# Batch 0's second quad of a windowed-attention kernel: own banks for its second score round, value units in two parts, and the first weight matrix loaded by 512 columns

## Chip, cores and metric

The kernel runs on one core of a Trainium2 chip. The metric is device microseconds (us) of one execution; of several executions the median counts. All inputs and the output lie in HBM, and the whole computation is one launch.

## What is computed

Two stages. The first is an attention of 8 batches x 8 heads, head size 64, with 512 local and 32 global positions. A local query sees the 32 global keys and the local keys at most 32 positions away; a global query sees everything. The second is a gated feed-forward over the 4352 resulting rows of 512 features.

```
s_g   = scale * q_g @ concat(k_g, k_l).T ;  out_g = softmax(s_g) @ concat(v_g, v_l)
s_ll  = scale * q_l @ k_l.T, kept where |i - j| <= 32 ;  s_lg = scale * q_l @ k_g.T
out_l = softmax(concat(s_lg, s_ll)) @ concat(v_g, v_l)
x     = concat(out_g, out_l), heads side by side: (8 * 544) x 512
h     = x @ w_in            # 512 x 2048
g     = h * sigmoid(1.702 * h)
out   = g @ w_out           # 2048 x 512
```

## The kernel before, in words

**Tiling.** Four heads of a batch form a quad, each head on 32 of the 128 partitions (its 64 features as pairs of bf16). Every batch has two quads; `a` is the first and `c` the second. Scores are computed keys by queries in four chunks of 128 keys; chunks 0 and 1 are score round 0, chunks 2 and 3 are round 1. In batch 0 the mask is added on TensorE: `B` (L327) multiplies a bias by an identity into the score banks, and `S` (L337) adds the scores of local keys to it. `gk` (L364) gives scores of global keys: for the global queries (32 columns) and, in `K` (L388), for all local queries (a bank of its own, `kb`). ScalarE takes the exponentials: `X` (L374) of the score banks, `XK` (L413) of `kb`. Then come three value units: unit 0 multiplies by ones (the denominators), units 1 and 2 by the two halves of the values. `ekU` (L417) opens a unit with the global keys, `U` (L428) adds the four local chunks. `Gm` (L443) does the global queries' rows, `eg` (L394) prepares its last operand. `R` (L459) turns the denominators into reciprocals on VectorE (transpose, reciprocal, transpose), and `XL` (L469) multiplies a value unit by them into `xL`, the feed-forward's input: quad `a` fills k chunks 0 and 1 of `xL`, quad `c` chunks 2 and 3. `G` (L472) finishes the global rows.

**Feed-forward.** `h_mm` (L582) multiplies a 128-column block `fc` of `w_in` (16 blocks, 4 k chunks each) by `xL`. Batch 0's first four blocks stand in one group of four banks: chunks 0 and 1 of all four first (L709), then, behind quad `c`'s `XL`, chunks 2 and 3 (L713). `tanh2`, `act4` and `h_step` (L595) follow, with Tanh on ScalarE and a multiply on VectorE. `o_mm` (L602) multiplies by `w_out`.

**PSUM.** There are eight banks. Four belong to the pool `psP` (L63), handed out in turn by `pbank` (L276): a new holder waits until the old holder's readers are done. The other four are two tiles of two banks each, `s0` and `s1`, handed out together by `spair` (L280); `bank(pair, j)` (L283) is one of the four. A pair of banks is one tile.

**Order.** The order on every engine is written out by hand; each engine runs its own list in order and waits where an operand or a buffer is not ready. L640 to L735 is batch 0. GpSimd (POOL) issues nearly all loads. `load_rest` (L251) is its list: values of batch 0, `w_in` as four DMAs of 512 KB (column half by column half, in each the rows of k chunks 0 and 1, then those of 2 and 3), two parts of `w_out`, six small mask copies, the loads of batch 1, two more parts of `w_out`, and so on. These DMAs share eight semaphores in turn, so each waits, before it is issued, for the landing of the eighth DMA before it. Later batches use the class `Wide` (L499) and the loop from L860, which the change does not touch.

Of the kernel before, what the change touches and what calls it, by code (L numbers as in the profile page):

```python
# [20 lines left out]
def kernel(  # L21
# [12 lines left out]
    nc = tc.nc  # L34

    B, H, Sl, D = q_l.shape
    Sg = q_g.shape[2]
    S = Sg + Sl
    n_tokens = B * S
    d_model = H * D  # L40
    d_ff = moe_w_in.shape[1]
    assert (B, H, Sl, Sg, D) == (8, 8, 512, 32, 64)
    W = 32
    scale = 1.0 / (D ** 0.5)
# [29 lines left out]
    def load(b, us=(0, 1), kq=True):  # L74
        if b not in loaded:
            loaded[b] = (ld.tile([128, 2, 16 * D], BF16, name="rk"),
                         ld.tile([128, 2, 16 * D], BF16, name="rq"))
        if kq:
            s = slice(us[0], us[-1] + 1)
            nc.gpsimd.dma_start(out=loaded[b][1][:, s], in_=qf[b][:, s])  # L80
            nc.gpsimd.dma_start(out=loaded[b][0][:, s], in_=kf[b][:, s])  # L81
# [8 lines left out]
    def load_v(b):  # L90
        if b == 2:
            nc.gpsimd.memset(v_view(b, 5)[:, :, :, :, D:], 1.0)
        vt = v_view(b, 5).rearrange("p u j c d -> p (u j) c d")
        vs, vg = (x[b].rearrange("h s d -> s h d") for x in (v_l, v_g))
        for c in range(5):
            n = 128 if c == 2 else 96
            nc.gpsimd.dma_start(out=vt[0:n, :, c, :D], in_=vs[FIRST[c] : FIRST[c] + n])  # L97
            if c != 2 and b > 1:
                nc.gpsimd.dma_start(out=vt[96:128, :, c, :D], in_=vg)  # L99

    def load_vg(b):
        nc.gpsimd.dma_start(out=v_view(b, 5).rearrange("p u j c d -> p (u j) c d")[96:128, :, 0, :D],
                            in_=v_g[b].rearrange("h s d -> s h d"))
# [16 lines left out]
    def load_g(lo, hi, names="kq"):  # L120
        for name, dst, src in (("k", rkg, kgf), ("q", rqg, qgf)):
            if name in names:
                nc.gpsimd.dma_start(out=dst[:, lo:hi, :], in_=src[:, lo:hi, :])
# [37 lines left out]
    for i in range(2):  # L161
# [3 lines left out]
        out=step, in_=step, pattern=[[1, 289]], compare_op=ALU.is_ge,  # L165
        fill=0.0, base=-97, channel_multiplier=-1,
    )
    w_in_sb = wts.tile([128, 2, NKC, d_ff // 2], BF16)
    w_out_sb = wts.tile([128, FC, d_model], BF16)
    w_in_r = moe_w_in.rearrange("(u p h) f -> u p h f", u=2, h=2)  # L170
# [30 lines left out]
    def near(t, c):  # L201
        lo = 0 if c else 2
        return t[:, :, lo : lo + WIN[c][1]]
# [13 lines left out]
    def make_mask(part):  # L217
        rnd, at, t0, t1, nr, base, rows = part
        src = band[:, base : base + 16 * nr].rearrange("p (r t) -> p t r", t=16)
        nc.gpsimd.tensor_copy(mask_at(rnd, at, t1 - t0, nr)[0:rows], src[0:rows, t0:t1])  # L220
# [19 lines left out]
    def load_v2(b):  # L240
        vp = v_l[b].rearrange("(u h) (c p) d -> u p h c d", u=2, p=128)
        for u in range(2):
            for p in (slice(0, 64), slice(64, 128)):
                nc.gpsimd.dma_start(out=v_view(b, 4)[p, u, :, :, :D], in_=vp[u, p])  # L244

    def load_w_out(g4):
        nc.gpsimd.dma_start(
            out=w_out_sb[:, 4 * g4 : 4 * g4 + 4, :].rearrange("p (g e) m -> p g (e m)", e=2),
            in_=w_out_r[:, 2 * g4 : 2 * g4 + 2, :])

    def load_rest():  # L251
        load_v2(0)
        half = d_ff // 2
        for part in range(2):
            for u in range(2):
                nc.gpsimd.dma_start(out=w_in_sb[:, part, 2 * u : 2 * u + 2, :],
                                    in_=w_in_r[u][:, :, part * half : (part + 1) * half])
        load_w_out(1)
        load_w_out(0)
        for part in MASKS:  # L260
            make_mask(part)
        load(1, (0,))
        load_g(2, 4)
        load(1, (1,))
        load_vg(1)
        load_w_out(2)
        load_w_out(3)
        load_v(1)
        load(2, (0,))
        load_g(4, 8)  # L270
        load(2, (1,))
# [4 lines left out]
    def pbank(name):  # L276
        return psP.tile([128, 512], F32, name=name, tag="p")


    def spair():  # L280
        return [psS.tile([128, 2, 512], F32, name="s4", tag="s%d" % i) for i in range(2)]

    def bank(pair, j):  # L283
        return pair[j // 2][:, j % 2, :]

    class Quad:
# [38 lines left out]


        def B(self, rnd, split=False, js=range(4)):  # L327
            if 0 in js:
                self.bk[rnd] = [pbank("s") for _ in range(4)] if split else self.spt(rnd)
            ps = self.bk[rnd] if split else [bank(self.bk[rnd], j) for j in range(4)]  # L330
            for c in (2 * rnd, 2 * rnd + 1):
                w = (40, 200, 36, 228)[c]
                for j in js:
                    nc.tensor.matmul(ps[j][:, w : w + 16 * WIN[c][1]], lhsT=ident, rhs=near(bias, c),
                                     start=(c == 2 * rnd), stop=False, skip_group_check=True)
# [49 lines left out]
            if rnd == self.gr:  # L385
                nc.scalar.activation(e[:, 2, RW:], bank(self.ps, 2)[:, RW : RW + 32], AF.Exp, scale=scale)

        def K(self, e=None):  # L388
            if e != 1:
                self.kb = pbank("kb")  # L390
            self.gk(self.kb, self.q[:, 4:20], e)


# [20 lines left out]
            self.ek = att.tile([128, Sl], BF16, name="ek")  # L414
            nc.scalar.activation(self.ek, self.kb, AF.Exp, scale=scale)

        def ekU(self, unit):  # L417
            ov = pbank("ov")
            self.st[unit] = ov
            for j in range(4):  # L420
                r = 32 * ((j + 1) % 4)
                p = slice(r, r + 32)
                lv = (ones32[p] if unit == 0 else
                      rvg[p, self.Q, :D].rearrange("p (w h) -> p w h", h=2)[:, :, unit - 1])
                nc.tensor.matmul(ov[32 * j : 32 * j + 32, :], lhsT=lv, rhs=self.ek[p],
                                 start=True, stop=False, skip_group_check=True)

        def U(self, unit):  # L428
            ov = self.st[unit]
            h = unit - 1  # L430
            for c in range(4):
                r0, nr = WIN[c]
                at = (40, 200, 36, 228)[c]
                for j in range(4):
                    lv = (ones32 if unit == 0 else
                          self.v[:, j, c, :D].rearrange("p (w h) -> p w h", h=2)[:, :, h])
                    nc.tensor.matmul(  # L437
                        ov[32 * j : 32 * j + 32, :].rearrange("p (t r) -> p t r", t=16)[:, :, r0 : r0 + nr],
                        lhsT=lv, rhs=self.E[c // 2][:, j, at : at + 16 * nr],
                        start=False, stop=(c == 3), skip_group_check=True,  # L440
                    )
# [140 lines left out]
    def h_mm(i, fc, hp, kcs):  # L582
        for kc in kcs:
            nc.tensor.matmul(hp[:, : width(i)], lhsT=w_in_c[:, fc // 8, kc, fc % 8 // 2, :, fc % 2],  # L584
                             rhs=(xL[i] if i < B else xG)[:, kc, :],
                             start=(kc == 0), stop=(kc == NKC - 1))
# [53 lines left out]
    a, c = Quad(0), Quad(1)  # L640
# [20 lines left out]
    cast_g32("k", rkg)  # L661
    transpose_g(0, 2, "k")
    load_rest()
    a.B(0)
    a.B(1, split=True)
# [8 lines left out]
    c.ext()  # L674
    c.Tk()
    c.B(0)
    a.K()
    a.XK()
    c.S(0, added=True)
    c.gg()  # L680
    c.X(0)
    a.eg()
    a.ekU(0)
    a.U(0)
    a.R()
    c.K()
    c.XK()
    a.ekU(1)
    a.U(1)
    a.XL(0)  # L690
    c.B(1, js=(0, 1))
    c.B(1, js=(2, 3))
    c.S(1, added=True)
    c.X(1)
    a.ekU(2)
    a.U(2)
    a.XL(1)
    a.Gm()
    gTs[0] = moe.tile([128, FC, TB], BF16, name="gT")
    pt = pts[0] = spair()  # L700
    c.ekU(0)
    c.ekU(1)
    c.U(0)
    c.R()
    c.U(1)
    c.ekU(2)
    c.U(2)
    c.eg()
    for fc in range(4):  # L709
        h_mm(0, fc, bank(pt, fc), (0, 1))  # L710
    c.XL(0)
    c.XL(1)
    for kc in (2, 3):  # L713
        for fc in range(4):
            h_mm(0, fc, bank(pt, fc), (kc,))
# [24 lines left out]
    a, c = nq[1]  # L740
# [28 lines left out]
    pt = spair()  # L769
# [7 lines left out]
    a, c = nq[2]  # L777
# [82 lines left out]
    for i in range(1, B):  # L860
        if i > 1:
            for fc in range(FC):
                h_step(i, fc)
        if i + 1 < B:
            phase_o(i)
# [36 lines left out]
```

## Time and profile before

| what | value |
|---|---|
| median of 3 runs | 301.46 us (301.28 to 302.13) |
| the profiled execution's own time | 302.02 us |
| its span, first to last instruction | 300.3 us |
| TensorE (PE) busy | 289.9 us (97%) |
| VectorE (DVE) busy | 219.0 us (73%) |
| ScalarE (ACT) busy | 165.1 us (55%) |
| GpSimd (POOL) busy | 78.0 us (26%) |
| mean granted TensorE clock | 0.998 |

So 1.7 us of the profiled execution lie outside the span, and that execution is 0.56 us above the median. All times inside the span count from its first instruction. In listings of the timeline each row gives the start, the length from the first start to the last end of a merged group, the engine (PEld is the weight loads of PE), the line, and how many instructions were merged; in brackets stands the idle time before the group and what ended it. Where a matmul's length is given, it is the time from its start to its modelled end; matmuls overlap, so a sequence is priced from start to start.

### The profile page before, as it was taken

To read this page: it belongs to the slowest core of one execution; us is meant where nothing else is said; L and a number is where in the kernel's file an instruction comes from. 1 tells how busy PE (TensorE), PEld (TensorE's weight loads), DVE (VectorE), ACT (ScalarE), POOL (GpSimd) and SP (SyncE) were. 2 spreads that over 40 slices of the span, in tenths; PEclk is the share of its full clock that TensorE was granted. 3 is DMA by queue.
4 is the path that set the end of the run, shared out by engine and by line. 5 is a ranking of instruction groups with operands and counts; after the bars stand their busy time and mean duration, and the time that the engine had idled before them with its cause. 6 is when DMAs were issued, how large, how long until landed. Compare 5 with 4: busy or idle time off the path is not lost.

```text
span 300.3 us, 8109 instructions
## 1 busy us (share of the span) xinstructions
PE 289.9 (97%) x3373; PEld 149.0 (50%) x3414; DVE 219.0 (73%) x446; ACT 165.1 (55%) x250; POOL 78.0 (26%) x126
## 2 busy tenths in 40 slices
PE   8889999999999999999999999999999999999994
PEld 4544446445454455445454455445554455456553
DVE  6668977979967887778967887778878866773310
ACT  4727465476547736477356745566446652663421
POOL 8942748728054001800072002500000000000000
PEclk9999999999999999999999999999999999999999
DMA  7999999994979312980289114900230022101123
GB/s 205 158 204 210 202 180 206 214 131 59 175 90 159 71 37 55 139 142 21 53 85 184 34 38 81 115 0 20 55 71 2 2 53 57 35 0 37 35 70 73
DMA packets 58373, 28.20 MB, mean 94 GB/s; under 512 B 47456, under 2 KB 47712, under 8 KB 58336
## 3 DMA queue, kind: packets, MB, share of 16 engines
q0 software_dynamic: 50496, 17.57, 51.8%
q1 hardware_dynamic: 7360, 9.45, 12.2%
q10 hardware_dynamic: 480, 0.66, 0.7%
q8 instruction: 27, 0.44, 0.6%
q14 instruction: 10, 0.08, 0.1%
HBM read 36.31 MB, written 8.91 MB: 151 GB/s over the span
## 4 chain that ended last, share of the span: by engine, by line
PE 84%; DVE 5%; DMA 4%; POOL 3%; ACT 2%; issue 1%; ACTq 0%; POOLq 0%
PE op L609 37%; PE hp L584 34%; PE s L529 6%; PE ov L555 5%; DMA w_in_sb<-in_moe_w_in_dram 4%; DVE gT L592 2%; POOL v L244 1%; ACT th L591 1%; DVE xL L470 1%; PE op L621 1%; PE s L584 1%; PE og L566 1%; DVE rs L465 0%; DVE sT L461 0%; ACT e L540 0%
## 5 line engine op out<-in xcount | busy, mean ns | idle before, releaser
L609 PE MATMUL op<-w_out_sb,gT 128*128 128x512 bf16 x497 | 119.4, 379 | 1.8 <-issue 0.3
L592 DVE SCALAR_TENSOR_TENSOR gT<-th,hp 128x512 bf16<-128x512 f32 (+1 forms) x140 | 91.0, 656 | 40.0 <-ACT th L591 38.8
L584 PE MATMUL hp<-xL,w_in_sb 128*128 128x512 bf16 x488 | 108.9, 379 | 1.3 <-DVE xL L470 0.4
L591 ACT ACTIVATE th<-hp 128x512 f32<-128x512 f32 (+1 forms) x140 | 79.7, 573 | 44.8 <-PE hp L584 40.3
L584 PEld LDWEIGHTS <-w_in_sb 128*128 128x128 bf16 x576 | 56.1, 98 | 66.9 <-issue 2.2
L609 PEld LDWEIGHTS <-gT 128*128 128x128 bf16 x528 | 49.3, 98 | 54.9
L623 ACT ACTIVATE ob<-op 128x512 f32<-128x512 f32 (+2 forms) x35 | 20.3, 587 | 67.6 <-PE op L609 65.1
L540 ACT ACTIVATE e<-s 128x1016 bf16<-128x1016 f32 (+1 forms) x56 | 53.3, 1005 | 7.4 <-PE s L529 7.1
L97 POOL DMA_DIRECT2D v<-in_v_l_dram x35 | 28.1, 809 | 92.5 <-PE og L566 88.3
L545 DVE TENSOR_TENSOR e<-e,mask 128x1712 bf16<-128x1712 bf16 (+1 forms) x27 | 28.1, 1041 | 5.2 <-ACT e L540 5.2
L461 DVE STREAM_TRANSPOSE sT<-ov 128x512 f32<-128x512 f32 x15 | 10.7, 716 | 14.9 <-PE ov L555 12.7
L470 DVE TENSOR_TENSOR xL<-ov,rs 128x512 bf16<-128x512 f32 x30 | 19.4, 686 | 1.9 <-PE ov L437 0.5
L529 PE MATMUL s<-q,kT 32*128 32x160 bf16 (+3 forms) x672 | 19.2, 243 | 0.0
L529 PEld LDWEIGHTS <-kT 32*128 32x128 bf16 x672 | 13.1, 94 | 12.0 <-issue 6.5
L99 POOL DMA_DIRECT2D v<-in_v_g_dram x24 | 14.2, 591 | 3.8 <-DMA rq<-in_q_l_dram 3.1
L503 DVE STREAM_TRANSPOSE kT<-rk 128x512 f32<-128x512 f32 x14 | 14.6, 1042 | 0.0
L465 DVE STREAM_TRANSPOSE rs<-rT 128x512 f32<-128x512 f32 x16 | 11.4, 711 | 0.6
L555 PE MATMUL ov<-e,v 128*32 128x128 bf16 (+3 forms) x624 | 11.8, 223 | 0.0
L312 DVE STREAM_TRANSPOSE q<-rq 128x512 f32<-128x512 f32 (+1 forms) x17 | 11.3, 667 | 0.1
L555 PEld LDWEIGHTS <-v 128*32 128x32 bf16 x672 | 10.5, 97 | 0.0
L584 PE MATMUL hp<-xG,w_in_sb 128*128 128x256 bf16 x64 | 9.6, 273 | 0.1
L81 POOL DMA_DIRECT2D rk<-in_k_l_dram x10 | 6.5, 648 | 3.6 <-DMA w_in_sb<-in_moe_w_in_dram 1.9
(99 smaller groups left out, 151.3 us busy)
## 6 DMA issues: line engine op xcount, KB each, us to landing
out_dram<-ob SPq DMA_DIRECT2D x132, 64.0 KB, 2.4
v<-in_v_l_dram POOLq DMA_DIRECT2D x28, 96.0 KB, 4.4
rq<-in_q_l_dram POOLq DMA_DIRECT2D x5, 512.0 KB, 7.6
rk<-in_k_l_dram POOLq DMA_DIRECT2D x5, 512.0 KB, 9.4
w_in_sb<-in_moe_w_in_dram POOLq DMA_DIRECT2D x4, 512.0 KB, 11.7
w_out_sb<-in_moe_w_out_dram POOLq DMA_DIRECT2D x4, 512.0 KB, 12.6
v<-in_v_l_dram POOLq DMA_DIRECT2D x11, 128.0 KB, 4.8
rq<-in_q_l_dram POOLq DMA_DIRECT2D x5, 256.0 KB, 8.6
```

Source lines behind the costliest of these rows:

```text
L97: nc.gpsimd.dma_start(out=vt[0:n, :, c, :D], in_=vs[FIRST[c] : FIRST[c] + n])
L470: nc.vector.tensor_mul(self.x[:, 2 * self.u + h, :], self.st[1 + h], self.st["rs"])
L503: nc.vector.transpose(flat[:, 0:Sl].rearrange("p (r t) -> p t r", t=16), loaded[self.b][0][:, self.u].bitcast(F32))
L529: nc.tensor.matmul(bank(self.ps, j)[:, at : at + n], lhsT=self.k[p, KEYS[c] : KEYS[c] + 128, e], rhs=self.q[p, lo:hi, r0 : r0 + nr, e], st ...
L540: nc.scalar.activation(self.E[rnd][:, 2 * i : 2 * i + 2, :n], self.ps[i][:, :, :n], AF.Exp, scale=scale)
L545: eng.tensor_mul(e, e, mask[:, rnd : rnd + 1, :n].to_broadcast([128, 4, n]))
L555: nc.tensor.matmul(ov[32 * j : 32 * j + 32, :].rearrange("p (t r) -> p t r", t=16)[:, t0:t1, r0 : r0 + nr], lhsT=lv, rhs=self.E[rnd][:, j, ...
L584: nc.tensor.matmul(hp[:, : width(i)], lhsT=w_in_c[:, fc // 8, kc, fc % 8 // 2, :, fc % 2], rhs=(xL[i] if i < B else xG)[:, kc, :], start=( ...
L591: nc.scalar.activation(th[:, :n], hp[:, :n], AF.Tanh, scale=0.851)
L592: nc.vector.scalar_tensor_tensor(gTs[i][:, fc, :n], in0=th[:, :n], scalar=1.0, in1=hp[:, :n], op0=ALU.add, op1=ALU.mult)
L609: nc.tensor.matmul(op, lhsT=gTs[i][:, fc, tci * 128 : tci * 128 + 128], rhs=w_out_sb[:, fc, :], start=(first and fc == 4 * f4), stop=(fc = ...
L623: nc.scalar.activation(ob[:, lo:hi], op[:, lo:hi], AF.Copy, scale=0.5)
```

## The change

It touches batch 0 and the `w_in` load only.

- `load_rest` loads `w_in` in six DMAs: columns 0 to 511 of k chunks 0 and 1, then of chunks 2 and 3 (256 KB each); columns 512 to 1023 the same way (256 KB each); then columns 1024 to 2047 in two DMAs of 512 KB as before.
- Quad `c`'s round 1 no longer uses the paired banks but four `psP` banks (`split=True`). Its bias is added in two steps: banks 0 to 2 before `a.ekU(0)`, bank 3 behind `a.U(1)`. The exponentials of that round are four instructions instead of two, and the global queries' scores are taken in round 1 (inside `S`) instead of by `gg` in round 0.
- `c.S(0)` moves ahead of `a.K`. `a`'s unit 0 goes into the bank of `a.kb`. The freed paired banks, under the new name `pt`, hold in this order: `c.kb`, `a`'s unit 1, `a`'s unit 2, `c`'s unit 0.
- Each of `c`'s value units is done in two parts: chunks 0 and 1 of all three units ahead of `a.Gm`, chunks 2 and 3 behind it. `c.R` stands behind the second part of unit 0. Both `a.XL` stand behind `a.U(2)`. `c.eg` moves behind `c.XL(1)`.

```
@@ load_rest
-        half = d_ff // 2
-        for part in range(2):
+        for part, lo, hi in ((0, 0, 512), (0, 512, 1024), (1, 0, 1024)):
             for u in range(2):
-                nc.gpsimd.dma_start(out=w_in_sb[:, part, 2 * u : 2 * u + 2, :],
-                                    in_=w_in_r[u][:, :, part * half : (part + 1) * half])
+                nc.gpsimd.dma_start(out=w_in_sb[:, part, 2 * u : 2 * u + 2, lo:hi],
+                                    in_=w_in_r[u][:, :, 1024 * part + lo : 1024 * part + hi])
@@ B
-            if 0 in js:
-                self.bk[rnd] = [pbank("s") for _ in range(4)] if split else self.spt(rnd)
+            if split:
+                self.bk.setdefault(rnd, []).extend(pbank("s") for _ in js)
+            elif 0 in js:
+                self.bk[rnd] = self.spt(rnd)
@@ K, ekU and U take a bank, or a list of chunks
-        def K(self, e=None):
+        def K(self, e=None, kb=None):
...
-                self.kb = pbank("kb")
+                self.kb = pbank("kb") if kb is None else kb
...
-        def ekU(self, unit):
-            ov = pbank("ov")
+        def ekU(self, unit, ov=None):
+            if ov is None:
+                ov = pbank("ov")
...
-        def U(self, unit):
+        def U(self, unit, cs=range(4)):
...
-            for c in range(4):
+            for c in cs:
@@ the order of batch 0
     c.B(0)
+    c.S(0, added=True)
     a.K()
     a.XK()
-    c.S(0, added=True)
-    c.gg()
     c.X(0)
     a.eg()
-    a.ekU(0)
+    c.B(1, split=True, js=(0, 1, 2))
+    a.ekU(0, a.kb)
     a.U(0)
     a.R()
-    c.K()
+    pt = spair()
+    c.K(kb=bank(pt, 0))
     c.XK()
-    a.ekU(1)
+    a.ekU(1, bank(pt, 1))
     a.U(1)
+    c.B(1, split=True, js=(3,))
+    c.S(1, split=True, added=True)
+    c.X(1)
+    a.ekU(2, bank(pt, 2))
+    a.U(2)
     a.XL(0)
-    c.B(1, js=(0, 1))
-    c.B(1, js=(2, 3))
-    c.S(1, added=True)
-    c.X(1)
-    a.ekU(2)
-    a.U(2)
     a.XL(1)
+    c.ekU(0, bank(pt, 3))
+    c.U(0, (0, 1))
+    for unit in (1, 2):
+        c.ekU(unit)
+        c.U(unit, (0, 1))
     a.Gm()
+    c.U(0, (2, 3))
+    c.R()
+    c.U(1, (2, 3))
+    c.U(2, (2, 3))
     gTs[0] = moe.tile([128, FC, TB], BF16, name="gT")
     pt = pts[0] = spair()
-    c.ekU(0)
-    c.ekU(1)
-    c.U(0)
-    c.R()
-    c.U(1)
-    c.ekU(2)
-    c.U(2)
-    c.eg()
     for fc in range(4):
         h_mm(0, fc, bank(pt, fc), (0, 1))
     c.XL(0)
     c.XL(1)
+    c.eg()
```

## The prediction

> **What bounds the kernel now.** I read the page first: PE is busy 97% of the span and carries 84% of the chain that ended last, so a change of order pays only where PE stands idle. The chain in order of time names the last such place that is not PE's or DVE's own pace, the second half of the first feed-forward block in batch 0:
>
> ```profile
> 9.99 11.03 DMA w_in_sb<-in_moe_w_in_dram
> 21.02 0.05 issue
> 21.07 1.90 PE s L584 x8
> ```
>
> The columns are start, length, what. A `w_in` load issued at 9.99 lands at 21.02, and PE goes on at 21.07. From there the chain is PE and DVE work to the end, released by each other and by no load; so a delay or gain at 21.07 goes through whole. The timeline from 8 to 29 us shows what stands ahead of it:
>
> ```profile
> 11.48 0.66 ACT L415 ACTIVATE ek<-kb 128x512 bf16<-128x512 f32 x1
> ...
> 11.96 1.74 ACT L384 ACTIVATE e<-s 128x856 bf16<-128x856 f32 x2
> ...
> 14.63 0.66 PE L351 MATMUL s<-q,kT 32*128 32x228 bf16 x16
> ...
> 15.34 1.66 ACT L384 ACTIVATE e<-s 128x856 bf16<-128x856 f32 x2 [1.06 <-PE s L351]
> ...
> 17.41 0.72 DVE L461 STREAM_TRANSPOSE sT<-ov 128x512 f32<-128x512 f32 x1 [0.63 <-PE ov L437]
> ...
> 18.59 1.67 PE L584 MATMUL s<-xL,w_in_sb 128*128 128x512 bf16 x7 [0.16 <-issue]
> ...
> 19.27 1.29 DVE L470 TENSOR_TENSOR xL<-ov,rs 128x512 bf16<-128x512 f32 x2
> ...
> 21.07 1.90 PE L584 MATMUL s<-xL,w_in_sb 128*128 128x512 bf16 x8 [0.81 <-DMA w_in_sb<-in_moe_w_in_dram]
> ```
>
> PE opens the block at 18.59; eight matmuls, 0.216 apart, would reach k chunk 2 at 20.31. Quad c's first `xL` ends at 19.96, its second at 20.56. So the load alone costs 0.76 us, and that is nearly all there is to win: from 9.99 to 18.59 PE idles only 0.27 at 12.19 (for XK) and 0.20 at 17.05 (for the second X). POOL's rows, whose waits end with the landing of the eighth DMA before, give the landings:
>
> ```profile
> 17.96 0.71 POOL L123 DMA_DIRECT2D rkg<-in_k_g_dram  x1 [1.05 <-DMA w_in_sb<-in_moe_w_in_dram]
> 21.31 0.71 POOL L123 DMA_DIRECT2D rqg<-in_q_g_dram  x1 [2.64 <-DMA w_in_sb<-in_moe_w_in_dram]
> 23.28 0.55 POOL L80 DMA_DIRECT2D rq<-in_q_l_dram  x1 [1.26 <-DMA w_in_sb<-in_moe_w_in_dram]
> 25.75 0.54 POOL L81 DMA_DIRECT2D rk<-in_k_l_dram  x1 [1.93 <-DMA w_in_sb<-in_moe_w_in_dram]
> ```
>
> The four 512-KB loads land at 17.7, 21.0, 23.0 and 25.5.
>
> **The loads.** Rows of 512 columns make 1024-byte packets. The trace's packet records of this queue show 128 bytes at 32 ns and 2048 at 173 ns. Bounds for 1024: 87 (bytes alone) and 173 (packets alone); I take 98, on the line between the rows, 0.33 us more per 512 KB. The third load then lands at 17.7 + 0.3 + half of (3.3 + 0.3) = 19.8, the fourth at 21.7, the two big ones at 23.7 and 26.1, all later loads 0.7 later. What needs them? In the built program the weight load of k chunk 1 waits for the third DMA and that of chunk 3 for the fourth: the ranges of a 512-column DMA over two chunks overlap with its neighbour's. So the split frees chunks 0 and 2 early and no more. By the schedule below PE wants the third load at 21.0 and the fourth at 23.9: covered by 1.2 and 2.2 us. The two added issues take POOL 0.70 us each, and the last `w_out` issue waits for the values' landing at 14.7; masks and batch 1's issues move back with it, but the masks are used near 40 us, and with six loads queued the DMA queue never runs dry. The nearest later need, the third `w_out` part, landed at 38.64 and was wanted near 39.65: 0.7 later is covered, the more so if PE is later too.
>
> The Trainium skill, "DMA: Bandwidth & Descriptors", section "Anatomy of one DMA", has 2.0 us fixed per DMA plus its bytes. Were that serial, two more DMAs would put the fourth load at some 25 us. The rows speak against it: queued loads land 2.0 to 3.3 us apart in all, so a fixed part hides behind the stream.
>
> **The order.** I follow PE by row durations; where one engine releases another, the rows show about 0.05 us (XK ends 12.14, PE starts 12.19).
> - To 10.55 nothing changes. `c.S(0)` takes 0.59, then `a.K` at 11.14, last end 0.62 later (10.55 to 11.18) at 11.76. XK 11.81 to 12.46 (0.65; it was 11.48 to 12.14). `c.X(0)` starts 0.48 behind XK's start, at 12.29; its first half ends 0.96 later at 13.25. The three banks of bias (6 matmuls, 0.5 us) fit beside XK, so they cost nothing; if XK were early they would cost up to 0.5. The `gg` taken out saves PE nothing, since it stood in the 0.27 wait, and comes back inside `S(1)`.
> - `a.ekU(0)` 12.51, `a.U(0)` 12.83 (0.33 and 0.42 from start to start). `c.K` needs X(0)'s first half, since it uses its bank: 13.30, end 13.92. XK 13.97 to 14.62.
> - **First new wait.** `a.ekU(1)` writes bank 1 of the pair whose bank 0 holds `c.kb`. A pair is one tile, and the built program makes this instruction wait for XK: 14.67. PE has had nothing from 13.6: 1.1 us. Everything of PE's list is queued behind it: `a.U(1)` 15.00, bias of bank 3 15.42, `c.S(1)` 15.66 (before: 14.63), global scores 16.25.
> - X(1) is now four instructions. In a's own X(1) they start 0.41 apart and the last ends 1.82 behind the first start; two big ones take 1.66. It starts at 16.37 (before 15.34) and ends at 18.19 (before 17.00).
> - `a.ekU(2)` 16.55, `a.U(2)` 16.87, end 17.37. `a.XL(0)` is done by 16.4 (R ends at 15.2). `a.XL(1)` 17.42 to 18.11 (0.69).
> - **Second new wait.** `c.ekU(0)` writes bank 3, the other half of the pair whose bank 2 XL(1) reads: the built program waits for XL(1), so 18.16. PE idles 0.9 us.
> - The value parts: per unit 0.32 for `ekU`, 0.10 for eight matmuls, 0.16 to change back (17.45 to 17.61): units 1 and 2 start 18.73 and 19.30, `Gm` 19.77, then the three second parts from 20.01, 0.16 each. The split adds some 0.3 us of changes. X(1)'s end at 18.19 is long past, so the wait for it is covered.
> - Unit 0 ends 20.34, sT starts 20.39 (before 17.41). From sT to the first XL took 1.86 (17.41 to 19.27): XL 22.25 to 22.94.
> - The block opens 0.39 behind the last value matmul, at 20.80, runs out of chunks 0 and 1 at 22.53 and waits 0.46 for XL. Chunk 2 starts at 22.99, chunk 3 at 23.85, XL(1) being done at 23.5.
>
> **The sum.** 22.99 against 21.07: +1.9 us. It is a path, not a sum of edits; its terms are XK and X(0) 0.33 later, the wait for `c.kb`'s XK, the wait for XL(1), the value parts ahead of `c.R`, and against it the 0.76 us of load wait, which goes; VectorE's XL is late in its place. Behind 22.99 the rows are the same as before, and no row behind 21.07 waits for a load that could take the shift up. The profiled execution took 302.02, so 303.9; it lies 0.56 above the median of 301.46, so I forecast 303.3 for the median. Unknown on this path: each of a dozen changes of tile shape on PE, 0.06 to 0.33 by the rows; together about 0.6 either way: 302.7 to 304.0.
>
> **Rivals.** (0.3%, 0.9 us, is about what a measurement of this kernel tells from no change.)
> 1. The pair-wide waits do not bite, because XK and XL are done early. Then `a.ekU(1)` is at 13.9, S(1) at 14.9, `c.ekU(0)` at 16.5, sT at 18.7, XL at 20.5 to 21.2, chunk 2 at 21.25: +0.2, 301.7. Against it: K itself waits for X(0), whose rows are known, and XK cannot start before K. 0.07.
> 2. Faster: the load was the only thing in the way and quad c's chain ends no later than now. The gain is 0.76, and the waits of 0.27 and 0.20 could go too: -1.2, 300.2. It decides for this if sT starts by 17.4; but X(1) would then have to end before 17, and its input `S(1)` stands behind one more XK. 0.04.
> 3. The small packets cost as much as big ones (173 ns). Loads three and four land at 23.5 and 26.0, PE waits for both, chunk 3 starts at 26.0 instead of 21.93: +4.1, 305.6. The 32 ns of the 128-byte packets speak against. 0.06.
> 4. PE's clock drops in the new gaps. The table by windows shows it granted in full (1.00) in every stretch up to 30 us, with idle pieces up to 0.81 between 8 and 23; the new ones are 1.1, 0.9 and 0.5. At half clock for 3 us of work, +1.5 more: 304.8. 0.03. The Trainium skill, "TensorE: Matmul & The Clock Gate", Part 1, drops the clock only after an idle window of about 3.4 us; by that there is none here, and the trace before, with no such gap, agrees as far as it goes.
>
> **How the numbers follow.** My forecast has 0.80. The range 302.0 to 304.6 takes the forecast's own 302.7 to 304.0, widens it by the spread of the runs shown (301.28 to 302.13), and leaves out rivals 1 to 4, 0.2 together. Slower by over 0.3% (over 302.4): the forecast but for a low tail, with rivals 3 and 4: 0.85. Within 0.3%: rival 1 and that tail: 0.10. Faster: rival 2 and a little of rival 1: 0.05.
>
> **What would show it.** Right: in the changed profile `a.ekU(1)` (L427) starts near 14.7 behind ACT's `ek` and `c.ekU(0)` near 18.2 behind DVE's `xL`, each with about 1 us of PE idle ahead; sT of quad c near 20.4; the chain carries DVE `xL` in place of the load, and chunk 2 starts near 23.0. Wrong: PE without gaps between 13 and 20, or L586 waiting for `w_in` again, or a later row that takes the shift up.

## The result, and the profile after

The changed kernel takes **304.75 us** (median of 4 runs, 304.41 to 304.98); the kernel before, with one more run than was shown, takes 301.66 (4 runs, 301.28 to 302.13). The ratio is 1.0097, with a 95% interval of 1.0077 to 1.0116: about 1% slower. The profiled execution took 304.41 with a span of 302.7, against 302.02 and 300.3.

From the page of the changed kernel, the span and the busy times:

```profile
span 302.7 us, 8113 instructions
...
PE 290.4 (96%) x3373; PEld 149.2 (49%) x3414; DVE 219.1 (72%) x446; ACT 165.5 (55%) x251; POOL 79.6 (26%) x128
```

These totals cannot tell where 2.4 us went: the change is one of order, and PE is still busy nearly all the time. The chain of waits can (start, length, what):

```profile
4.26 5.57 DMA rk<-in_k_l_dram
9.85 1.06 DVE kT L307
...
10.96 0.66 PE s L352 x16
11.62 0.59 PE kb L371 x8
12.23 0.60 ACT ek L416
12.82 1.55 ACT e L385 x2
14.38 0.56 ACT ek L416
...
14.97 0.40 PE s L427 x4
...
18.21 0.40 PE s L427 x4
...
20.44 0.73 DVE sT L463
...
22.29 0.70 DVE xL L472
23.04 1.89 PE s L586 x8
```

In the chain before, a `w_in` load released the second half of the feed-forward block at 21.07. Now no `w_in` load stands in the chain. What stands there is quad c's own work: `c.S(0)` behind the landing of `rk` and its transpose, `a.K` behind `c.S(0)`, ScalarE's exponentials in a row (`a.XK`, `c.X(0)`, `c.XK`), a wait of PE for ScalarE's `ek` at 14.97, a wait for VectorE's `xL` at 18.21, the value parts up to `sT` at 20.44, and VectorE's `xL` in the place where the load was. Chunk 2 starts at 23.04.

The timeline of the same stretch shows what PE idles for (in brackets: the idle time ahead of the row and who ended it):

```profile
14.33 0.60 ACT L416 ACTIVATE ek<-s 128x512 bf16<-128x512 f32 x1
...
14.97 0.40 PE L427 MATMUL s<-ek,rvg 32*32 32x512 bf16 x4 [0.69 <-ACT ek L416]
...
17.47 0.69 DVE L472 TENSOR_TENSOR xL<-s,rs 128x512 bf16<-128x512 f32 x1 [0.88 <-PE s L439]
...
18.21 0.40 PE L427 MATMUL s<-ek,ones 32*32 32x512 bf16 x4 [0.80 <-DVE xL L472]
...
20.46 0.72 POOL L123 DMA_DIRECT2D rqg<-in_q_g_dram  x1 [1.04 <-DMA w_in_sb<-in_moe_w_in_dram]
...
20.85 1.67 PE L586 MATMUL s<-xL,w_in_sb 128*128 128x512 bf16 x7 [0.16 <-issue]
...
22.29 1.29 DVE L472 TENSOR_TENSOR xL<-ov,rs 128x512 bf16<-128x512 f32 x2
23.04 1.89 PE L586 MATMUL s<-xL,w_in_sb 128*128 128x512 bf16 x8 [0.51 <-DVE xL L472]
```

At 14.97 the `ek` that PE waits for is that of `c.XK`, not of its own operand: `a.ekU(1)` uses `a`'s exponentials of 12.2 us. At 18.21 it waits for `a.XL(1)`, which reads the other bank of the pair. The loads are out of the way: by the trace the four 512-column loads landed at 15.8, 17.2, 18.4 and 20.2, and POOL's issue, which waits for the last of these, went out at 20.46, while PE reaches chunk 3 only at 23.9.

One thing has to be known to read this block: its sixteen matmuls are not all on record in every trace. Here the row at 20.85 has seven of the first eight. The weight loads (PEld), which are complete here, show that the first matmul is the missing one. A later profile of the kernel before (e12) has all sixteen, and there the first weight load and the first matmul start together:

```profile
18.41 1.41 PEld L584 LDWEIGHTS <-w_in_sb 128*128 128x128 bf16 x8
18.41 3.90 PE L584 MATMUL s<-xL,w_in_sb 128*128 128x512 bf16 x16
```

In the first profile before, the weight loads of the block start at 18.36, and in the changed kernel at 20.62:

```profile
18.36 1.41 PEld L584 LDWEIGHTS <-w_in_sb 128*128 128x128 bf16 x8
```

```profile
20.62 1.63 PEld L586 LDWEIGHTS <-w_in_sb 128*128 128x128 bf16 x9
```

So the block opened at 18.36 before, not at 18.59, and opens at 20.62 now. With eight matmuls 0.216 apart PE would have been at chunk 2 at 20.09, so in that execution the load held PE up by 0.98 and not by 0.76.

Where the 2.4 us between the two spans lie: chunk 2 starts 1.97 later (21.07 to 23.04) and the last group of matmuls 1.89 later (292.55 to 294.44). From the start of chunk 2 to the start of the last matmul it takes 274.8 to 275.0 us in all fourteen profiles of this case, so what is lost at chunk 2 arrives whole at the end. The rest, some 0.5 us, lies behind the last matmul: the last two copies of the output (L623 before, L625 after) start 1.34 us apart before and 1.74 after. Between them ScalarE issues two output DMAs (ACTq). In the kernel before:

```profile
295.39 0.83 ACTq L631 DMA_DIRECT2D out_dram<-ob  x2
...
296.27 0.33 ACT L623 ACTIVATE ob<-op 128x192 f32<-128x192 f32 x1 [0.91 <-PE op L621]
```

In the changed kernel:

```profile
297.28 0.93 ACTq L633 DMA_DIRECT2D out_dram<-ob  x2
...
298.55 0.33 ACT L625 ACTIVATE ob<-op 128x192 f32<-128x192 f32 x1 [1.30 <-PE op L623]
```

Before, the copy starts 0.05 behind the end of these issues (296.22 to 296.27), and after, 0.34 (298.21 to 298.55). This is not a matter of the single execution: it is 0.05 in all four profiles with the order before (the first, e1, e5 and e12), and 0.33 or 0.34 in all ten with the changed order. So the change costs nearly 0.3 us here as well; why, no run shows. What is left behind the start of the last copy differs from execution to execution, between 3.8 and 4.8 us in the fourteen profiles.

### The profile page after: what moved, and what is told of

Its sections match the earlier page's. It is cut to its first block, busy times and chain, and to the rows that moved or that the text cites. A ratio compares the mean times of both kernels' runs of the same rounds, so it can differ in the third digit from the quotient of the medians.

```text
span 302.7 us, 8113 instructions
## 1 busy us (share of the span) xinstructions
PE 290.4 (96%) x3373; PEld 149.2 (49%) x3414; DVE 219.1 (72%) x446; ACT 165.5 (55%) x251; POOL 79.6 (26%) x128
## 4 chain that ended last, share of the span: by engine, by line
PE 87%; DVE 4%; ACT 2%; DMA 2%; issue 2%; POOL 1%; ACTq 0%; DVEq 0%; POOLq 0%
PE op L611 38%; PE hp L586 34%; PE s L531 6%; PE ov L557 5%; DVE gT L594 2%; DMA rk<-in_k_l_dram 2%; ACT th L593 1%; PE op L623 1%; PE og L568 1%; PE s L586 1%; ACT e L385 1%; DVE xL L472 0%; PE s L439 0%; PE s L352 0%; PE s L557 0%
## 5 line engine op out<-in xcount | busy, mean ns | idle before, releaser
L625 ACT ACTIVATE ob<-op 128x512 f32<-128x512 f32 (+2 forms) x35 | 20.3, 587 | 68.6 <-PE op L611 65.7
L472 DVE TENSOR_TENSOR xL<-ov,rs 128x512 bf16<-128x512 f32 x28 | 18.0, 685 | 1.4
L463 DVE STREAM_TRANSPOSE sT<-ov 128x512 f32<-128x512 f32 x13 | 9.3, 716 | 12.7 <-PE ov L557 12.7
L80 POOL DMA_DIRECT2D rq<-in_q_l_dram x10 | 6.6, 664 | 3.0 <-DMA w_in_sb<-in_moe_w_in_dram 3.0
```

The lines of the kernel that those rows point to most:

```text
L472: nc.vector.tensor_mul(self.x[:, 2 * self.u + h, :], self.st[1 + h], self.st["rs"])
L625: nc.scalar.activation(ob[:, lo:hi], op[:, lo:hi], AF.Copy, scale=0.5)
```

## The experiments

All times are medians; ratios are against the kernel before, run on the same chip at the same time. An interval reaches some 0.2%, or 0.6 us, to either side. So the repairs of one cause alone (e6, e7, e8 and e10, 1.0058 to 1.0080) are not told apart in time from the repeat of the changed kernel (1.0078), and what each is worth is read from the rows of its profile; e3, e9 and e11 (1.0008 to 1.0018) are clearly below it. e1 to e4 share one set of runs of the kernel before (301.86), e5 to e8 another (301.50), e9 to e12 a third (301.85).

**The theory** was that the order costs the time: two waits that arise because two banks are one tile (a pair), the move of `c.S(0)` ahead of `a.K`, and the value units in two parts. **The rivals**: the loads cost it (small packets), or the clock falls in the new gaps. The clock needs no experiment. The table by windows of the changed kernel (stretch, then busy us of PE, PEld, DVE, ACT and POOL, then the granted clock, DMA share and GB/s) has PE busy for only 3.2 of 4 us, and the clock at 1.00:

```profile
12.00:16.00 4.00, 3.17 (x64) 1.54 (x63) 1.78 (x4) 2.70 (x4) 3.88 (x8) 1.00 1.23 169
16.00:20.00 4.00, 3.21 (x95) 1.61 (x97) 1.28 (x2) 1.81 (x4) 3.21 (x8) 1.00 1.18 200
```

**e1: only the loads.** The kernel before with the six loads in place of four:

```diff
-        half = d_ff // 2
-        for part in range(2):
+        for part, lo, hi in ((0, 0, 512), (0, 512, 1024), (1, 0, 1024)):
```

> The kernel before with the six w_in loads alone, its order untouched. My theory (the loads do no harm, the order does): in the changed profile the first four loads landed at 15.8, 17.2, 18.4 and 20.2, so nothing of the first feed-forward block waits for a load; chunk 2 starts at 20.3 instead of 21.07 and the kernel is 0.7 us faster than before, about 0.9975 of it. Rival (the loads cost something, by small packets or by two more issues on POOL): no change or slower than before, above 1.000.

Measured: 301.64 (12 runs), ratio 0.9994 [0.9977, 1.0011]. The load wait is gone, but the gain of 0.7 that was expected for it did not come. The timeline of e1 shows PE going through chunk 2 without a break, as one group (the first of the sixteen matmuls has no record again; chunk 2 starts at 19.85):

```profile
18.34 3.40 PE L583 MATMUL s<-xL,w_in_sb 128*128 128x512 bf16 x15 [0.16 <-issue]
```

So the loads alone neither cost nor win anything that can be measured, and the 0.76 us that the first profile seemed to offer was in question.

**e2: only the order.** The changed kernel with the four old loads (e1's edit the other way round).

> The changed kernel with the four w_in loads of before. My theory: chunk 2 still starts near 23.0, held by quad c's xL, and the load that lands at 21.0 is covered; the time is that of the changed kernel within 0.3 us. Rival (the loads carry part of the 3 us): at least 0.6 us faster than the changed kernel.

Measured: 304.18 (6 runs), ratio 1.0075 [1.0053, 1.0096]; chunk 2 at 23.06. The whole loss is there without the loads.

**e3: neither pair-wide wait.** The same work on PE in the same order; only the banks that three value units write are exchanged, so that no unit shares a pair with a bank whose reader is late:

```diff
-    a.ekU(1, bank(pt, 1))
+    a.ekU(1, bank(pt, 2))
...
-    a.ekU(2, bank(pt, 2))
+    a.ekU(2, bank(pt, 1))
```

> The changed kernel with its units in other banks of the two pairs: a's unit 1 in bank 2, a's unit 2 in bank 1, c's unit 0 in bank 3. The first new wait is then for the second half of X(0) (14.4 in the changed profile) instead of XK (14.9), the second for the first xL (done by 16.6) instead of the second. My theory (the two pair-wide waits carry most of the delay): c.ekU(0) starts near 16.8 instead of 18.2, chunk 2 near 21.5 instead of 23.0, and the time is 1.5 us below the changed kernel, some 303.2. Rival (the later X(1) of four instructions and the value parts carry it): X(1) ends at 18.0 to 18.5 in any case, chunk 2 stays above 22.5, and less than 0.6 us is won.

Measured: 302.58 (12 runs), ratio 1.0018 [1.0001, 1.0034]. In the profiled execution chunk 2 started at 22.25, later than expected, because `rk` landed at 10.47 and `c.S(0)` with it at 11.59. From `c.S(0)` to chunk 2 it took 10.66, against 12.08 in the changed kernel: 1.42 less, where 1.5 was expected. The rows of `c.S(0)`, `a.ekU(1)` and `c.ekU(0)`, the last two without a wait:

```profile
11.59 0.66 PE L352 MATMUL s<-q,kT 32*128 32x200 bf16 x16 [1.16 <-DVE eg L397]
...
15.06 0.40 PE L427 MATMUL s<-ek,rvg 32*32 32x512 bf16 x4
...
17.44 0.40 PE L427 MATMUL s<-ek,ones 32*32 32x512 bf16 x4
```

**e4: the changed kernel again**, unchanged, beside e1 to e3.

> The changed kernel once more, unchanged. Its profiled execution was 2.4 us longer than that of the kernel before, of which 1.9 at the start and 0.4 behind the last matmuls, while the medians are 3.1 apart. If the two profiled executions were chance draws from the ends of their spreads: this profile has its chunk 2 later than 23.04 or other gaps, and the ratio stays at 1.010. If the ratio is nearer 1.007, the medians of four runs were the chance.

Measured: 304.45 (6 runs), ratio 1.0078 [1.0056, 1.0101]. `c.S(0)` at 10.82, chunk 2 at 22.89, 12.07 apart. e3 is 1.9 us below it, and e2 level with it within the intervals.

**e5: the kernel before again**, with a profile, to see whether its load wait recurs.

> The kernel before once more, unchanged, for a second profiled execution. The six loads alone brought nothing in the median (ratio 0.999), although their profile has chunk 2 at 19.85 instead of 21.07; and with the four loads in the changed order the second load landed at 19.4, not at 21.0. If the wait of 0.8 us for that load was a chance of the one profiled execution, it lands near 19.5 to 20.3 here, chunk 2 starts at 20.4 or earlier and PE has no wait for w_in. If the wait is the rule, the landing is again near 21.

Measured: 301.88 (10 runs) against 301.50, ratio 1.0012 [0.9996, 1.0028]: the same kernel. From the timeline of this execution:

```profile
18.51 3.40 PE L584 MATMUL s<-xL,w_in_sb 128*128 128x512 bf16 x15 [0.16 <-issue]
...
19.81 0.71 POOL L123 DMA_DIRECT2D rqg<-in_q_g_dram  x1 [1.55 <-DMA w_in_sb<-in_moe_w_in_dram]
```

The matmuls of the block are one group without a wait, again without a record of the first; the weight loads start at 18.27, and chunk 2 starts inside the group at 20.02. POOL's row, which waits for the second `w_in` load, is at 19.81; it was at 21.31 in the first profile. By the trace the load landed at 19.53 instead of 21.02. The two executions are of the same kernel.

**e6: the second wait alone taken away** (`c.ekU(0)` writes bank 0, whose pair had been read by 16.7):

```diff
-    c.ekU(0, bank(pt, 3))
+    c.ekU(0, bank(pt, 0))
```

> The changed kernel with c's unit 0 in bank 0 instead of bank 3 of the pairs, so that it waits for a's first xL (done by 16.6) and not for the second; the first new wait stays. Counted from the start of c.S(0), which moves with a load's landing, chunk 2 came 12.1 us later in the changed kernel and 10.7 in the one with both waits eased. My theory: 11.3 here, 0.8 us below the changed kernel, about 303.7. Rival (X(1)'s end carries it): unchanged at 12.1.

Measured: 303.34 (4 runs), ratio 1.0060 [1.0041, 1.0080]; chunk 2 at 22.25, 11.21 behind `c.S(0)` at 11.04. In its timeline `c.ekU(0)` has no wait any more; `sT` starts 9.48 behind `c.S(0)` in the changed kernel and 8.61 here:

```profile
11.04 0.66 PE L352 MATMUL s<-q,kT 32*128 32x200 bf16 x16 [1.03 <-DVE eg L397]
...
17.43 0.40 PE L427 MATMUL s<-ek,ones 32*32 32x512 bf16 x4
...
19.65 0.72 DVE L463 STREAM_TRANSPOSE sT<-s 128x512 f32<-128x512 f32 x1 [1.41 <-PE s L439]
```

The edit has a side effect: the feed-forward block, whose first bank is in that pair too, now waits for `sT` and opens at 20.42. Chunk 2 is held by `xL` all the same. The same holds for e7.

**e7: the first wait alone taken away.** `a.ekU(1)` writes bank 2 and `a.ekU(2)` bank 1, as in e3, and `c.ekU(0)` bank 0, so that it still shares a pair with the unit that `a.XL(1)` reads.

> The changed kernel with a's unit 1 in bank 2, a's unit 2 in bank 1 and c's unit 0 in bank 0: a.ekU(1) waits for the second half of X(0) instead of XK, and c.ekU(0) still waits for the second xL. My theory: 0.55 us earlier than in the changed kernel, 11.55 us from c.S(0) to chunk 2, about 303.9. Rival: unchanged at 12.1.

Measured: 304.02 (4 runs), ratio 1.0080 [1.0056, 1.0104]; chunk 2 at 22.57, 11.6 behind `c.S(0)`. The timeline:

```profile
14.44 0.40 PE L427 MATMUL s<-ek,rvg 32*32 32x512 bf16 x4
...
17.75 0.40 PE L427 MATMUL s<-ek,ones 32*32 32x512 bf16 x4 [0.87 <-DVE xL L472]
```

`a.ekU(1)` starts 0.53 earlier without a wait, the second wait stays. By the profile the first wait is worth 0.5; the ratio's interval is too wide to show half a microsecond.

**e8: `a.K` and `a.XK` ahead of `c.S(0)`**, as in the kernel before, all else as changed:

```diff
-    c.S(0, added=True)
     a.K()
     a.XK()
+    c.S(0, added=True)
```

> The changed kernel with a.K and a.XK ahead of c.S(0) again, as before the change; banks and loads as changed. In the changed profiles c.S(0) starts 1.1 us behind the landing of quad c's keys (9.7 to 10.5), because nothing stands ahead of it on PE; with a.K ahead it has until 11.1. My theory (this move put the landing on the path and XK behind it): XK starts near 11.5 instead of 12.2, c.XK ends near 14.2 instead of 14.9, chunk 2 near 22.3, and the time is 0.7 us below the changed kernel, about 303.8. Rival (the move is harmless, as the prediction took it, but for 0.3 us): 0.3 us or less.

Measured: 303.39 (4 runs), ratio 1.0062 [1.0044, 1.0080]. `a.K` fills PE until `c.S(0)` at 11.09, and everything that hangs on `a.XK` is earlier:

```profile
14.31 0.40 PE L427 MATMUL s<-ek,rvg 32*32 32x512 bf16 x4 [0.70 <-ACT ek L416]
...
17.55 0.39 PE L427 MATMUL s<-ek,ones 32*32 32x512 bf16 x4 [0.80 <-DVE xL L472]
```

Both waits are still there, each 0.66 earlier than in the changed kernel (14.97, 18.21), and chunk 2 starts at 22.37. `rk` landed early in this execution, at 9.06, so e8 alone does not show that `a.K` hides a later landing. e9 and e11, which have the same order, do: there it landed at 9.76 and 9.73, and `c.S(0)` still starts right behind `a.K`, at 11.17 and 11.06.

**e9: e8 and e3 together** (`a.K` first and neither pair-wide wait).

> Both repairs in the changed kernel: a.K and a.XK ahead of c.S(0), and the units in banks 2, 1 and 3 so that neither pair-wide wait bites. Chunk 2 stood at 20.2 in the second profile of the kernel before and at 22.4 with a.K moved alone. My theory (three causes that add up: the load's landing ahead of XK, the wait for XK, the wait for the second xL): a.ekU(1) near 13.7, c.ekU(0) near 16.1, sT near 18.3, chunk 2 near 20.9; 0.6 us above the kernel before, ratio 1.002. Rival (the value parts and the four exponentials alone cost a microsecond): chunk 2 above 21.4, ratio above 1.004.

Measured: 302.63 (10 runs), ratio 1.0017 [1.0002, 1.0031]. Every row came within 0.1 of what was expected:

```profile
13.80 0.40 PE L427 MATMUL s<-ek,rvg 32*32 32x512 bf16 x4
...
16.17 0.40 PE L427 MATMUL s<-ek,ones 32*32 32x512 bf16 x4
...
18.40 0.72 DVE L463 STREAM_TRANSPOSE sT<-s 128x512 f32<-128x512 f32 x1 [1.34 <-PE s L439]
...
21.00 1.89 PE L586 MATMUL s<-xL,w_in_sb 128*128 128x512 bf16 x8 [0.52 <-DVE xL L472]
```

In time it is not below e3 (302.63 and 302.58). That the third cause adds to the other two is thus seen in the rows alone.

**e10: the value units whole again** (units 1 and 2 undivided behind `c.R`, unit 0 still in two parts with `a.Gm` between), all else as changed:

```diff
-    for unit in (1, 2):
-        c.ekU(unit)
-        c.U(unit, (0, 1))
     a.Gm()
     c.U(0, (2, 3))
     c.R()
-    c.U(1, (2, 3))
-    c.U(2, (2, 3))
+    for unit in (1, 2):
+        c.ekU(unit)
+        c.U(unit)
```

> The changed kernel with c's value units whole: unit 0 in two parts with a.Gm between, its reciprocals right behind, units 1 and 2 undivided behind that. My theory (the six part groups ahead of c.R delay sT by a microsecond, but PE then needs that time behind it): sT near 19.4 instead of 20.4, chunk 2 held by PE's own work at 22.7 instead of 23.0; 0.4 us below the changed kernel. Rival (sT alone sets chunk 2): 1.0 us below, chunk 2 near 22.0.

Measured: 303.47 (4 runs), ratio 1.0058 [1.0041, 1.0074]. The timeline:

```profile
18.24 0.40 PE L427 MATMUL s<-ek,ones 32*32 32x512 bf16 x4 [0.80 <-DVE xL L472]
...
19.27 0.72 DVE L463 STREAM_TRANSPOSE sT<-s 128x512 f32<-128x512 f32 x1 [1.08 <-PE s L439]
...
20.64 3.63 PE L586 MATMUL s<-xL,w_in_sb 128*128 128x512 bf16 x16
```

The units that were first parts in front of `c.R` cost 1.2 us there: `sT` starts 1.03 behind `c.ekU(0)`, and 2.23 with the parts. Only 0.7 of it reaches chunk 2 (22.38), since PE then opens the block no sooner than 20.64 and is itself what is late.

**e11: e9 and e10 together**; what stays of the change is the loads, the early `c.S(1)`, the own banks, the exponentials of round 1 in four instructions, and unit 0 in two parts.

> Both repairs and whole units. PE's own work then sets the time: U(0)'s second part waits for X(1)'s end near 17.2, units 1 and 2 follow, the block opens near 19.1, chunk 2 near 20.8: like the kernel with both repairs, 0.6 us above the kernel before. Rival (sT alone sets chunk 2): 20.1, no slower than before.

Measured: 302.10 (10 runs), ratio 1.0008 [0.9995, 1.0021]: no difference from the kernel before that can be told, though the 0.6 us that were expected lie inside the interval. The timeline:

```profile
17.25 0.31 PE L439 MATMUL s<-e,ones 128*32 128x192 bf16 x5 [0.18 <-ACT e L380]
...
17.60 0.72 DVE L463 STREAM_TRANSPOSE sT<-s 128x512 f32<-128x512 f32 x1 [0.65 <-PE s L439]
...
18.99 3.63 PE L586 MATMUL s<-xL,w_in_sb 128*128 128x512 bf16 x16
```

`sT` is back at 17.60 (17.41 before) and the block runs without a break from 18.99 (18.36 before, by its first weight load), with chunk 2 at 20.73.

**e12: the kernel before a third time**, a single run, for the landing again.

> A third profile of the kernel before. If the late landing (21.0, chunk 2 at 21.07) was a chance of the first profiled execution: landing of the second w_in load below 20.3 and chunk 2 near 20.2, as in the second profile. If it is common: landing near 21 again.

Measured: 301.57 (1 run), span 299.9. From its chain of waits:

```profile
10.56 9.80 DMA w_in_sb<-in_moe_w_in_dram
20.36 0.05 issue
20.41 1.90 PE s L584 x8
```

The weight load of chunk 2, from the timeline:

```profile
20.40 1.41 PEld L584 LDWEIGHTS <-w_in_sb 128*128 128x128 bf16 x8 [0.59 <-DMA w_in_sb<-in_moe_w_in_dram]
```

The landing, 20.36, lies between the other two and between the two cases of the expectation. The load is in the chain again. The block opened at 18.41, so PE would have been at chunk 2 at 20.14; the load holds it up by 0.27, against 0.98 in the first profile.

## Why the prediction was right or wrong

**Direction and mechanism were right.** Both waits came where they were forecast and for the reasons given. The path came out close to the reckoning; that its end came out to 0.05 is in part luck, as the missed step below shows:

| step | forecast | measured | what the runs showed |
|---|---|---|---|
| `c.S(0)` in `a.K`'s place | 10.55 | 10.96 | waits for the transpose behind `rk` |
| first wait, `a.ekU(1)` | 14.67 | 14.97 | worth 0.54 (e3) |
| second wait, `c.ekU(0)` | 18.16 | 18.21 | worth 0.86 (e6), 1.40 with the first (e3) |
| `sT` | 20.39 | 20.44 | parts ahead of `c.R`: 1.2 (e10) |
| chunk 2 | 22.99 | 23.04 | 21.00 with both waits gone and `a.K` first (e9), 20.73 with whole units too (e11) |
| third and fourth load | 19.8, 21.7 | 18.4, 20.2 | covered, as forecast |

The worth of a wait is read from `c.S(0)`: to `a.ekU(1)` 4.01 in the changed kernel and 3.47 in e3; to `c.ekU(0)` 7.25, 6.39 in e6 and 5.85 in e3. The two savings add up exactly.

**The mis-sized term was "against it the 0.76 us of load wait, which goes".** It was read off one profiled execution, and from 18.59, where the second matmul of the block starts; from the first it was 0.98 there. Nor does it recur: the second `w_in` load landed at 21.02 there, and at 19.53 and 20.36 in the two repeats, where it holds PE up not at all and by 0.27; and e1, which takes this wait away and leaves the order, is worth 0.2 us (1 − 0.9994, of 301.86), at most 0.7 by its interval. Against the repeats (20.02, 20.41) the changed kernel's chunk 2 (23.04, and 22.89 in e4) is 2.5 to 3.0 late, and not 1.9. Nearly 0.3 more comes at the last copy of the output, where the prediction had "Behind 22.99 the rows are the same as before". The ratio of e4 says 2.35 and that of the first comparison 2.9; these intervals overlap (1.7 to 3.0 and 2.3 to 3.5 us).

**The same execution misled a second time**, in the step from 303.9 to the median: "it lies 0.56 above the median of 301.46, so I forecast 303.3". The surplus belonged to that execution of the kernel before, with its late load; the changed kernel, which has no load on its path, has no reason to inherit it. Its profiled execution lies 0.34 below its own median. Of the 1.45 between forecast and median, this step makes 0.90 (0.56 + 0.34), and 0.5 is 304.41 against 303.9, nearly all of it behind the last matmul. The median of 304.75 lies just above the range of 302.0 to 304.6; as a difference from the kernel before (3.09, on 301.66) it lies just inside (3.14, on 301.46). Not all runs of the kernel before without that wait are as fast as e5's profile: e1's, in which the load is covered, spread from 301.13 to 302.57. So how much of the 0.56 was the load was not settled.

**The missed step**: "To 10.55 nothing changes." With `c.S(0)` put ahead of `a.K`, all of quad c stands behind `rk`, whose landing moves from 9.06 to 10.47 between executions. Before, `a.K` stood in front and hid a landing as late as 10.36 (e5, where the weight loads of the block start at 18.27, against 18.36 in the first profile). Here it made 0.41. It did not show in the sum because as much came back in small pieces: the halves of `c.X(0)` were quicker than taken (first half done 0.88 behind its start instead of 0.96), XK took 0.60 instead of 0.65, and the global scores ran beside `a.ekU(2)`, which started 0.62 behind `c.S(1)` instead of 0.89.

**Two idle times were misread.** The prediction has PE idle for 1.1 us ahead of the first wait's end and for 0.9 ahead of the second's. Its own rows give 0.75 (`c.K` ends at 13.92, PE goes on at 14.67) and 0.79 (17.37 to 18.16); the trace has 0.69 and 0.80. The forecast times do not hang on this.

**The rivals.** The first (the waits do not bite) and the second (faster) fell with the chain. Of the third (packets as dear as big ones) nothing holds: the trace has 98 ns for 1024 bytes, the value taken, and the fourth load landed at 20.2, not 26.0. The two added DMAs cost no time of their own that shows: in the changed kernel's trace the four 256-KB loads landed 1.2 to 1.7 us apart. The last of them landed at 20.2 there, and between 18.6 and 21.2 in the ten profiles with six loads; the same megabyte in two loads landed between 19.4 and 21.0 in four profiles. The Trainium skill, "DMA: Bandwidth & Descriptors", section "Anatomy of one DMA", gives 2.0 us fixed per DMA; read as a serial cost, that would have put this load near 25 us, by an estimate (21.0 and twice 2.0). The measurement decides: in this queue, with loads waiting behind each other, the fixed part does not add up. The fourth (the clock) fell with the table by windows: 1.00 with gaps of 0.69 and 0.80. The Trainium skill, "TensorE: Matmul & The Clock Gate", Part 1, asks for a much longer idle window, and the trace agrees as far as gaps of this length go.

**Open**: why the same loads land up to 1.5 us apart in two executions, why ScalarE's last copy starts nearly 0.3 us later with the changed order, and the difference between 1.0078 and 1.0097 for one kernel. No version tried here beats the kernel before.

## What to carry to other kernels

A buffer that shares a tile with another shares its waits, so "a bank of its own" is only its own if nothing else in its tile is still being read: here 0.5 and 0.9 us, and gone by exchanging bank numbers. Before a wait in the profile is booked as gain, see whether it recurs in a second execution and whether the rows that it is counted from are complete, and do not carry the profiled execution's distance from the median over to a kernel that no longer has what caused it. A step moved forward takes its input's landing time with it: look at what the step that it overtakes was hiding.

## What was not expected of the hardware

The landing of one and the same load varies by as much as 1.5 us from execution to execution. `rk`, issued near 4.26, landed between 9.06 (e8) and 10.47 (e3); the second `w_in` load of the kernel before landed between 19.53 and 21.02. And what the small packets cost does not show: 98 ns for 1024 bytes against 173 for 2048 would make a megabyte 13% slower (2 x 98 / 173), or 0.7 us by the prediction's count, but it landed at 18.6 to 21.2 in small packets (ten profiles, mean 20.0) and at 19.4 to 21.0 in large ones (four profiles, mean 20.1). A cost of this size is within the spread, so it is not shown to be absent either.
